# One batch's attention in whole float32, and a PSUM tile for each half of the experts' transposed rows

## The chip, the cores and the metric

The kernel runs on 1 core of one Trainium2 chip. The metric is the device time of one execution in microseconds (us); lower is better. A difference of 0.2% of the time is about what a measurement can tell from no change.

## The reference

```python
# 4 batches, 8 heads, 576 positions, head size 64
q_rot, k_rot = (rotate(q), rotate(k))                     # rotary embedding
scores = scale * np.matmul(q_rot, k_rot.transpose(0, 1, 3, 2))
scores = scores - np.max(scores, axis=-1, keepdims=True)
attn = np.exp(scores)
attn = attn / (np.sum(attn, axis=-1, keepdims=True) + 1e-09)
x = np.matmul(attn, v)                                    # then as 2304 rows of 512
# dense layer, 512 -> 2048 -> 512
h = x @ w_in
x = np.maximum(0.01 * h, h) @ w_out
# eight experts, each row goes to one
logits = xn @ en.T / tau                                  # rows and expert vectors of length 1
expert_idx = np.argmax(logits, axis=1)
for e in range(E):
    mask = expert_idx == e
    h = np.maximum(x[mask] @ w1[e], 0.0)
    out[mask] = gate_w[mask, None] * (h @ w2[e])
```

Inputs and output are float32.

## The kernel before, in words

**Parted numbers.** Nearly all matmuls take a float32 value as two narrower ones, a high part and the rest (low), and add up three products of the parts. ScalarE (ACT) makes a high part with a copy, VectorE (DVE) the low part with a subtraction.

**Attention.** The 16 pairs of heads (`g`: batch `g // 4`) have 9 units each (`u`), 144 in all. A unit is 128 queries of one head, the ninth one 64 queries of both heads. `prep(g)` makes a pair ready: it takes the sums of squares of q, k and v (`square`, ACT), turns q and k by the rotary tables (`rope_s2`, `rope_c2`, `add2`, DVE), sets scales, parts q and k into float16 (`hi`, `lo`) and has a DMA transpose put them into `stk`, d on the partitions. `prep_v` parts v. A unit then takes these steps: `a_scores` (PE, four float16 matmuls of 288 columns into the PSUM tile `S`), `a_max` (DVE, scaled scores to `E` with the row's extreme), `a_exp` (ACT), then the turned weights: `a_turn` (five PE transposes of `E` into the PSUM tile `acc`), `a_turned_hi` (ACT) and `a_turned_lo` (DVE) part them into `PT`; `a_pv` (15 float16 matmuls of 64 or 65 columns, 30 for the ninth unit) and `a_fin`. From the unit at which the dense layer starts, a DMA transposes the weights instead (`a_hi`, `a_lo`, `a_transpose`).

**Order.** The program is written in the order in which it runs on each engine. `step(i)` writes one step: the scores of unit i + 1, the maximum of unit i, the exponential and the turning of unit i - 1, the products of unit i - `LAG`. `ORDER1` is the order of the letters in a step ahead of the dense layer (X: `a_max`, E: `a_exp`, V: `a_pv`, T: `a_turn`, H and L: high and low part, C: `a_scores`, s and x: background pieces). Background jobs are the decoding of the dense weights (32 slices of 512 KB, `weights`), the preparation of the next pair and, later, x. A slice gets a piece in only when each engine's budget is above zero; `RATE1` adds to the budget at each step.

**Phases.** After a start of about 31 us, units 0 to 36 run with the decoding of the dense weights beside them. At unit 37 batch 0 is through and the dense layer's units (`m_s1`, `m_s2`) join. From about 780 us the experts run in 20 blocks of 128 rows (`e_block`). One block has `e_h` (24 PE matmuls, next block), `e_split` (the two weights parted again: 8 ACT copies, 8 DVE subtractions), `e_xt`, `e_relu`, `e_o` (24 matmuls), `e_weigh` and `e_tr`, which transposes the next block's hidden rows: four PE transposes for each half z, an ACT copy to `hth` and a DVE subtraction to `htl`. Both halves are written into one two-bank PSUM tile `acc`, and the framework tracks waits by the tile.

The lines to follow are L519 (`a_max`), L524 (`a_exp`), L543 (`a_turn`), L548 and L553 (high and low part of the turned weights), L567 (`a_pv`), L509 and L513 (`a_scores`), L427 and L493 (low parts in the preparation), and L917, L919, L925 (`e_tr`).

Of the kernel before, what the change touches and what calls it, by code (L numbers as in the profile page):

```python
# [32 lines left out]
LAG = 4  # L33
XTB = 2
# [4 lines left out]
EARLY = 2  # L39
# [8 lines left out]
RATE1 = dict(A=2.3, V=2.5)  # L48
# [44 lines left out]
def attention_moe_kernel(ctx: ExitStack, tc: tile.TileContext, qkv, w_in, w_out, emb, tau, w1, w2,  # L93
# [257 lines left out]
    v16s = [qkp.tile([128, 9, 2, 130], F16, name=f"v16{i}") for i in range(2)]  # L351
    pairs = {}
    xrow = {}

    def load(g, z):
        raws[g, z] = qkp.tile([128, z, 2, 5, 64], F32, name=f"raw{z}")
        for t in ([slice(0, 2)] if g else [slice(0, 1), slice(1, 2)]) if z == 2 else [slice(2, 3)]:
            if z == 2:
                M.loaded = M.tick
            if (g, z, t.start) == (0, 2, 1):  # L360
                nc.sync.dma_start(out=tab, in_=rope)
            nc.sync.dma_start(out=raws[g, z][:, t.start % 2:t.start % 2 + t.stop - t.start], in_=qkv[g, :, t])

    def prep(g):
        i0 = 9 * (g - 1)
        v16 = v16s[g % 2]
        raw, rawv = raws.pop((g, 2)), raws.pop((g, 1))[:, 0]
        sq = small.tile([128, 3], F32, name="sq3")
        cs, sn = tab[:, 0], tab[:, 1]
        if g:  # L370
            t4 = qkp.tile([128, 4, 5, 64], F32, name="t2", tag="stg")
        else:
            t2 = [mp.tile([128, 2, 5, 64], F32, name=f"t2{t}", tag="xT", bufs=XTB) for t in range(2)]

# [12 lines left out]

        def add(t):
            nc.vector.tensor_tensor(out=raw[:, t], in0=raw[:, t], in1=t2[t], op=ALU.add)

        r4 = raw.rearrange("p t h c d -> p (t h) c d")

        def rope_s2(z):
            o, i = 32 * z, 32 - 32 * z
            nc.vector.tensor_tensor(out=t4[:, :, :, o:o + 32], in0=r4[:, :, :, i:i + 32],
                                    in1=sn[:, :, o:o + 32].unsqueeze(1).to_broadcast([128, 4, 5, 32]), op=ALU.mult)

        def rope_c2():
            xf = raw.rearrange("p t h c d -> p (t h) (c d)")
            nc.vector.tensor_tensor(out=xf, in0=xf, in1=cs.rearrange("p c d -> p (c d)").unsqueeze(1).to_broadcast([128, 4, 320]), op=ALU.mult)  # L400

        def add2():
            rf = raw.rearrange("p t h c d -> p (t h c d)")
            nc.vector.tensor_tensor(out=rf, in0=rf, in1=t4.rearrange("p a c d -> p (a c d)"), op=ALU.add)
# [17 lines left out]
        def hi(out, t):  # L422
            nc.scalar.activation(out=out, in_=raw[:, t], func=AF.Copy, scale=s3[:, t:t + 1])

        def lo(out, t, high):
            for h in range(2):
                nc.vector.scalar_tensor_tensor(out=out[h], in0=raw[:, t, h], scalar=s3[:, t:t + 1], in1=high[:, h], op0=ALU.mult, op1=ALU.subtract)  # L427

        if g == 0:
            rope_s(1, nc.gpsimd)  # L430
            rope_s(0, nc.vector)
            for t in range(3):
                square(t)
            rope_c(0)
            add(0)
            pb = ps_x()
            nc.tensor.matmul(pb[:, 0:3], lhsT=ones, rhs=sq, start=True, stop=True)
            s3 = scales(pb)
            s2, qhi, khd, qlo, klo = stacks()
            hi(qhi, 0)  # L440
            rope_c(1)
            add(1)
            hi(khd[:, :, :, 0:64], 1)
            lo(qlo, 0, qhi)
            nc.vector.tensor_copy(out=khd[:, :, :, 64:128], in_=khd[:, :, :, 0:64])
            lo(klo, 1, khd[:, :, :, 0:64])
        else:
            yield Piece(A=0.93, V=0.73, at=max(i0 - EARLY, 0), tick=M.loaded + TLOAD)
            square(0)
            rope_s2(0)  # L450
            yield Piece(A=0.93, V=0.73)
            square(1)
            rope_s2(1)
            yield Piece(A=0.93, V=1.4)
            square(2)
            rope_c2()
            yield Piece(V=1.4)
            add2()
            pb = yield from total(sq, 3)
            yield Piece(must=True, V=0.6)  # L460
            s3 = scales(pb)
            s2, qhi, khd, qlo, klo = stacks()
            yield Piece(A=0.82)
            hi(qhi, 0)
            yield Piece(A=0.82, V=0.8)
            hi(khd[:, :, :, 0:64], 1)
            lo(qlo, 0, qhi)
            yield Piece(V=1.2)
            lo(klo, 1, khd[:, :, :, 0:64])
            nc.vector.tensor_copy(out=khd[:, :, :, 64:128], in_=khd[:, :, :, 0:64])  # L470
# [11 lines left out]
        pairs[g] = (stk, s3, sc, v16, zq[g % 2] if zq else None)  # L482
        if g + 1 < 4 * B:
            load(g + 1, 2)
        vjobs.append(Job(prep_v(g, v16, rawv, s3)))

    def prep_v(g, v16, rawv, s3):
        vh, vl = (v16[:, 0:5, :, o:o + 64].rearrange("p c h d -> p h c d") for o in (64, 0))
        yield Piece(A=0.82, at=9 * (g - 1) + LAG)
        nc.scalar.activation(out=vh, in_=rawv, func=AF.Copy, scale=s3[:, 2:3])  # L490
        yield Piece(V=0.75)
        for h in range(2):
            nc.vector.scalar_tensor_tensor(out=vl[:, h], in0=rawv[:, h], scalar=s3[:, 2:3], in1=vh[:, h], op0=ALU.mult, op1=ALU.subtract)  # L493
# [7 lines left out]
    def a_scores(g, u):  # L501
# [32 lines left out]
    def a_transpose(p):  # L534
        pt = ptp.tile([128, 10, 128], F16, name="PT")
        nc.sync.dma_start_transpose(out=pt[:, 0:9], in_=p)
        return pt, False
# [8 lines left out]
    def a_turned_hi(tf):  # L546
        pt = ptp.tile([128, 10, 128], F16, name="PT")
# [770 lines left out]
```

## Time and profile before

| | |
|---|---|
| time, median of 3 runs | 1089.99 us (1089.51 to 1091.2) |
| the profiled execution: its own time | 1091.79 us |
| its span | 1089.9 us |
| busy: PE matmul | 953.3 us (87%) |
| busy: PE weight load | 751.4 us (69%) |
| busy: DVE | 816.4 us (75%) |
| busy: ACT | 688.7 us (63%) |
| mean granted TensorE clock | 0.92 |

Busy times are shares of the whole span. The phases have different limits, so a share over the span does not say what a phase waits for.

### The profile page before, as it was taken

How to read it: one execution, taken by the hardware profiler on the slowest of the kernel's cores; microseconds unless marked ns; L12 is line 12 of the kernel's file. 1: busy time of each engine (PE TensorE's matmuls, PEld its weight loads, DVE VectorE, ACT ScalarE, POOL GpSimd, SP SyncE). 2: the span in 40 equal slices, each digit the busy share in tenths (PEclk: the TensorE clock that was granted, in tenths of full speed). 3: DMA queues.
4: the chain of work that ended last, by engine and by line, in shares of the span. 5: the costliest groups of instructions: out<-in, count | busy, mean ns of one | idle time of the engine just before them, and what ended most of it. 6: DMA issues, size and time to landing. Idle time of an engine off the chain costs nothing. (4 is left out here: it accounts for less than half of the span.)

```text
span 1089.9 us, 20159 instructions
## 1 busy us (share of the span) xinstructions
PE 953.3 (87%) x7427; PEld 751.4 (69%) x7427; DVE 816.4 (75%) x1663; ACT 688.7 (63%) x1105; POOL 53.3 (5%) x52
## 2 busy tenths in 40 slices
PE   1687787899997889998899999999987888888886
PEld 0354554576776677887788888888775777777774
DVE  6998888899877877897788765224757887777782
ACT  6767666677656655666675655232447777777772
POOL 1000000000000000000000000000003111111100
PEclk9956555699999889999999999999998999999998
DMA  8534426477567777667877844001430111133280
GB/s 243 154 79 155 134 66 188 87 160 150 111 136 159 122 150 152 139 129 155 151 136 142 143 78 85 20 21 42 162 115 31 49 40 39 39 99 124 75 292 13
DMA packets 232425, 124.41 MB, mean 114 GB/s; under 512 B 202616, under 2 KB 212216, under 8 KB 232321
## 3 DMA queue, kind: packets, MB, share of 16 engines
q1 hardware_dynamic: 229120, 113.10, 45.0%
q0 software_dynamic: 3200, 9.97, 2.6%
q8 instruction: 60, 0.98, 0.4%
q14 instruction: 45, 0.36, 0.1%
HBM read 120.04 MB, written 10.49 MB: 120 GB/s over the span
## 5 line engine op out<-in xcount | busy, mean ns | idle before, releaser
L248 PEld LDWEIGHTS <-wi 128*128 128x128 f16 x1920 | 171.4, 99 | 26.2 <-issue 4.2
L278 PE MATMUL acc<-wo,gh 128*128 128x512 f32 x576 | 156.9, 416 | 6.1 <-ACT gh L262 6.0
L519 DVE TENSOR_SCALAR_CACHE_REDUCE E<-S,sc 128x576 f32<-128x576 f32 x144 | 117.0, 813 | 38.5 <-PE S L511 27.6
L278 PEld LDWEIGHTS acc<-wo,gh 128*128 128x128 f32 x576 | 106.8, 195 | 31.2 <-ACT gh L262 8.5
L255 ACT ACTIVATE g<-h 128x512 f32<-128x512 f32 x72 | 43.0, 597 | 129.2 <-DVE gl L266 56.1
L567 PEld LDWEIGHTS <-PT 128*128 128x128 f16 (+1 forms) x2280 | 91.7, 107 | 34.7 <-issue 22.9
L248 PE MATMUL h<-xT,wi 128*128 128x256 f16 (+1 forms) x1152 | 113.4, 257 | 0.9 <-DMA xT<-x 0.9
L567 PE MATMUL o<-v,PT 128*128 128x65 f16 (+3 forms) x2280 | 105.9, 204 | 7.8 <-DMA PT<-P 7.8
L524 ACT ACTIVATE E<-E,amx 128x576 f32<-128x576 f32 x144 | 110.4, 767 | 3.6 <-DVE E L519 3.2
L509 PE MATMUL S<-stk 128*128 128x288 f16 (+1 forms) x320 | 94.5, 322 | 15.1 <-DVE E L519 14.4
L532 DVE SCALAR_TENSOR_TENSOR P<-E,P 128x576 f16<-128x576 f32 x108 | 81.2, 752 | 18.5 <-ACT P L528 18.2
L528 ACT ACTIVATE P<-E 128x576 f16<-128x576 f32 x108 | 73.8, 684 | 29.1 <-DMA PT<-P 25.8
L248 PE MATMUL h<-xt,wi 128*128 128x256 f16 x768 | 90.8, 276 | 0.4 <-DMA xt<-x 0.4
L278 PE MATMUL acc<-wo,gl 128*128 128x512 f32 x288 | 79.1, 397 | 0.0
L258 DVE SCALAR_TENSOR_TENSOR g<-h,g 128x512 f32<-128x512 f32 x72 | 49.5, 688 | 29.0 <-ACT g L255 28.9
L266 DVE TENSOR_TENSOR gl<-g,gh 128x512 fp32r<-128x512 f32 x72 | 49.4, 686 | 25.4 <-ACT gh L262 15.4
L543 PE MATMUL acc<-idn,E 128*128 128x128 f32 x180 | 46.2, 421 | 22.3 <-ACT E L524 15.9
L278 PEld LDWEIGHTS acc<-wo,gl 128*128 128x128 f32 x288 | 55.4, 193 | 12.8 <-DVE gl L266 0.3
L917 PE MATMUL acc<-idn,hs 128*128 128x128 f32 x160 | 25.7, 284 | 35.8 <-DVE htl L925 34.8
L935 PE MATMUL h<-w,hth 128*128 128x512 f32 x176 | 55.4, 396 | 0.0
L262 ACT ACTIVATE gh<-g 128x512 fp32r<-128x512 f32 x72 | 44.4, 617 | 15.1 <-PE acc L278 14.2
L925 DVE TENSOR_TENSOR htl<-acc,hth 128x512 fp32r<-128x512 f32 x40 | 27.5, 689 | 33.4 <-ACT hth L919 33.4
(237 smaller groups left out, 1869.0 us busy)
## 6 DMA issues: line engine op xcount, KB each, us to landing
rb<-in_w SPq DMA_DIRECT2D x78, 512.0 KB
ra<-in_w SPq DMA_DIRECT2D x76, 512.0 KB
raw<-in_qkv SPq DMA_DIRECT2D x15, 640.0 KB
raw<-in_w_in SPq DMA_DIRECT2D x16, 512.0 KB
raw<-in_w_out SPq DMA_DIRECT2D x16, 512.0 KB
raw<-in_qkv SPq DMA_DIRECT2D x18, 320.0 KB
x2s<-x SPq DMA_DIRECT2D x18, 256.0 KB
v<-v SPq DMA_DIRECT2D x16, 162.5 KB
```

What stands on the lines that cost most here:

```text
L248: nc.tensor.matmul(m.h[:, c0:c1], lhsT=wi[:, a, c, 128 * f:128 * f + 128], rhs=xT[j][:, 4 * b_ + c, 0:c1 - c0], start=(n == 0), stop=(n == ...
L258: nc.vector.scalar_tensor_tensor(out=m.g, in0=m.h, scalar=0.01, in1=m.g, op0=ALU.mult, op1=ALU.max)
L266: nc.vector.tensor_tensor(out=m.gl, in0=m.g, in1=m.gh.bitcast(F32), op=ALU.subtract)
L278: nc.tensor.matmul(M.acc[:, t], lhsT=g_[:, tt], rhs=wo[:, a, f], start=(f == 0 and n == 0), stop=(f == NF - 1 and n == 2))
L509: nc.tensor.matmul(ps[o:o + m, n, 0:288], lhsT=stk[:, h, c0:c0 + m], rhs=stk[:, 2 + h, ks], start=True, stop=False)
L519: nc.vector.tensor_scalar(out=e[:, 0:S].rearrange("p (a b) -> p a b", a=2), in0=ps[:, :, 0:288], scalar1=pairs[g][2][:, 1:2], scalar2=None ...
L524: nc.scalar.activation(out=e[:, 0:S], in_=e[:, 0:S], func=AF.Exp, scale=-1.0, bias=mx)
L528: nc.scalar.activation(out=p[:, 0:576], in_=e[:, 0:S], func=AF.Copy, scale=TWO15)
L532: nc.vector.scalar_tensor_tensor(out=p[:, 576:1152], in0=e[:, 0:S], scalar=TWO15, in1=p[:, 0:576], op0=ALU.mult, op1=ALU.subtract)
L543: nc.tensor.transpose(tf[:, 128 * i:128 * i + 128], e[:, 128 * i:128 * i + 128], idn)
L567: nc.tensor.matmul(o[ob:ob + m, 256 * h:256 * h + w], lhsT=pt[:, i, q0:q0 + m], rhs=v16[:, j, h, c:c + w], start=(n == 0), stop=(n == len( ...
L935: nc.tensor.matmul(OP[kk], lhsT=h_[:, c, :], rhs=wt[a][c // 2][:, 512 * (c % 2):512 * (c % 2) + 512], start=(n == 0), stop=(n == len(todo) ...
```

## The change

For the pairs of the first batch (`g < WHOLE`, 36 units) q, k, v and the exponentials stay float32: `prep_whole` takes the place of `prep`, without squares, scales, parts and DMA transpose. It turns q and k with ten PE transposes and three ACT copies. `load_values` loads v as it is, with the column of ones beside it. A score is one float32 matmul, the turned weights are one ACT copy (`a_turned`), and `a_pv` has 5 float32 matmuls. The layout of q, k, v in memory is changed (blocks of positions ahead of heads), so the rotary products have other shapes for all pairs. `RATE1` is raised from 2.3 and 2.5 to 2.4 and 2.7. In `x_done` a doubling moves into the scale of the square. In `e_tr` each half has a one-bank PSUM tile of its own (`ps_o`, two buffers).

```diff
+WHOLE = 4
-RATE1 = dict(A=2.3, V=2.5)
+RATE1 = dict(A=2.4, V=2.7)
...
+    def load_values(g):
+        yield Piece(at=9 * (g - 1) + LAG)
+        v = values[g] = stp.tile([128, 1170], F32, name="v32", tag="v")[:, 0:650].rearrange("p (c h x) -> p c h x", c=5, h=2)
+        nc.gpsimd.memset(v[:, :, :, 64:65], 1.0)
+        nc.sync.dma_start(out=v[:, :, :, 0:64], in_=qkv[g, :, 2])
...
+    def ropes(raw):
+        t4 = qkp.tile([128, 2, 5, 2, 64], F32, name="t2", tag="stg")
+        cs, sn = (tab[:, i].unsqueeze(2).to_broadcast([128, 5, 2, 64]) for i in range(2))
+
+        def rope_s(t):
+            for z in range(2):
+                o, i = 32 * z, 32 - 32 * z
+                nc.vector.tensor_tensor(out=t4[:, t, :, :, o:o + 32], in0=raw[:, t, :, :, i:i + 32], in1=sn[:, :, :, o:o + 32], op=ALU.mult)
+
+        def rope_c(t):
+            nc.vector.tensor_tensor(out=raw[:, t], in0=raw[:, t], in1=cs, op=ALU.mult)
...
+    def prep_whole(g):
+        i0 = 9 * (g - 1)
+        raw = raws.pop((g, 2))
+        qk = stp.tile([128, 1600], F32, name="qk", tag="stk")[:, 0:1280].rearrange("p (t x) -> p t x", t=2)
+
+        def turn(t, pt):
+            for c in range(4):
+                nc.tensor.transpose(pt[:, 128 * c:128 * c + 128], raw[:, t, c].rearrange("p h d -> p (h d)"), idn)
...
+        def keep(t, pt):
+            nc.scalar.activation(out=qk[:, t, 0:512], in_=pt, func=AF.Copy)
...
+            yield Piece(V=0.85, at=max(i0 - EARLY, 0), tick=M.loaded + TLOAD)
+            rope_s, rope_c, add = ropes(raw)
+            rope_s(0)
+            yield Piece(V=0.85)
+            rope_s(1)
+            yield Piece(V=1.5)
+            rope_c(0)
+            rope_c(1)
+            yield Piece(V=1.4)
+            add(slice(0, 2))
+            for t in range(2):
+                yield Piece(x=True)
+                pt = ps_x()
+                turn(t, pt)
+                yield Piece(must=True, A=0.6)
+                keep(t, pt)
...
             for h, c0, m, o in todo:
                 hr = slice(64 * h, 64 * h + 64)
+                if g < WHOLE:
+                    nc.tensor.matmul(ps[o:o + m, n, 0:288], lhsT=stk[hr, 0, c0:c0 + m], rhs=stk[hr, 1, ks], start=True, stop=True)
+                    continue
...
-    def a_turned_hi(tf):
-        pt = ptp.tile([128, 10, 128], F16, name="PT")
-        nc.scalar.activation(out=pt[:, 0:5].rearrange("p i q -> p (i q)"), in_=tf, func=AF.Copy, scale=TWO15)
-        return pt, True
-
-    def a_turned_lo(tf, pt):
-        hi, lo = (pt[:, z:z + 5].rearrange("p i q -> p (i q)") for z in (0, 5))
-        nc.vector.scalar_tensor_tensor(out=lo, in0=tf, scalar=TWO15, in1=hi, op0=ALU.mult, op1=ALU.subtract)
+    def a_turned(tf):
+        pt = ptp.tile([128, 5, 128], F32, name="ET", tag="PT")
+        nc.scalar.activation(out=pt.rearrange("p i q -> p (i q)"), in_=tf, func=AF.Copy)
+        return pt
...
+        if g < WHOLE:
+            todo = [(i, i, 0, 65) for i in range(5)]
...
-        pa = ps_a()
         for z in range(2):
-            pt = pa[:, z]
+            pt = ps_o()
...
-        turn = not (M.unit or m_ready())
+        turn = prv and units[i - 1][0] < WHOLE
```

In PE's queue, one step of the units of batch 0 (S is the score tile, acc the turned exponentials, o the products, E the exponentials) stood so; 15 pairs of a weight load and a product follow, of which two stand here:

```order
L543 MATMUL acc<-idn,E_117 128x128 x5
L509 LDWEIGHTS stk
L509 MATMUL S<-stk 128x288
L513 LDWEIGHTS stk
L513 MATMUL S<-stk 128x288
L509 LDWEIGHTS stk
L509 MATMUL S<-stk 128x288
L513 LDWEIGHTS stk
L513 MATMUL S<-stk 128x288
L567 LDWEIGHTS PT
L567 MATMUL o<-v_122,PT 128x65
```

Now the same place has these rows, with the transposes of the next pair's q or k (raw) among them:

```order
L583 MATMUL acc<-idn,E_117 128x128 x5
L404 MATMUL t<-idn,raw_177 128x128 x2
L547 MATMUL S<-qk 128x288 x2
L603 MATMUL o<-v_129,ET 128x65 x5
L583 MATMUL acc<-idn,E_118 128x128 x5
```

Four score matmuls have become two and 15 products five, all in float32, and ten transposes for each pair are new on PE.

In DVE's queue, the steps between two maxima (L519) at units 4 to 6 stood so (raw, wi, wo: decoding of the dense weights; v: low part of v; PT: low part of the turned weights):

```order
L519 TENSOR_SCALAR E_117,amx<-S,sc 128x576
L493 SCALAR_TENSOR_TENSOR v_123<-raw_203,ps,v_123 128x5x64 x2
L553 SCALAR_TENSOR_TENSOR PT<-acc,PT 128x640
L86 TENSOR_SCALAR pt<-t 128x1
L87 TENSOR_SCALAR ps<-pt 128x1
L88 TENSOR_SCALAR uw<-pt 128x1
L519 TENSOR_SCALAR E_118,amx<-S,sc 128x576
L226 SCALAR_TENSOR_TENSOR wi<-raw_310,ps,wi 128x4x128
L192 SCALAR_TENSOR_TENSOR raw_348<-raw_348 128x512
L553 SCALAR_TENSOR_TENSOR PT<-acc,PT 128x640
L194 SCALAR_TENSOR_TENSOR raw_348<-raw_348 128x512
```

Now there stand at units 3 to 5, with L559 as the maximum:

```order
L559 TENSOR_SCALAR E_118,amx<-S 128x576
L193 SCALAR_TENSOR_TENSOR raw_293<-raw_293 128x512
L195 SCALAR_TENSOR_TENSOR raw_293<-raw_293 128x512
L559 TENSOR_SCALAR E_117,amx<-S 128x576
L193 SCALAR_TENSOR_TENSOR raw_316<-raw_316 128x512
L195 SCALAR_TENSOR_TENSOR raw_316<-raw_316 128x512
L87 TENSOR_SCALAR pt<-t 128x1
L88 TENSOR_SCALAR ps<-pt 128x1
L89 TENSOR_SCALAR uw<-pt 128x1
L559 TENSOR_SCALAR E_118,amx<-S 128x576
```

The parting of the turned weights and of v is gone from a step, and the decoding stands a little earlier among the units.

In PE's queue at an expert block's `e_tr` (the end of `e_o`, the two halves, the start of `e_h`), with what each row waits for, stood:

```order
L935 MATMUL h<-v2h_10178,htl 128x512
L917 MATMUL acc<-idn,hs 128x128 [waits Activation_49]
L917 MATMUL acc<-idn,hs 128x128 x3
L917 MATMUL acc<-idn,hs 128x128 [waits DVE_49]
L917 MATMUL acc<-idn,hs 128x128 x3
L900 MATMUL S<-v1h_10167,exh 128x512 [waits Activation_49]
```

Now there stand:

```order
L970 MATMUL h<-v2h_9650,htl 128x512
L952 MATMUL o<-idn,hs 128x128 [waits Activation_49]
L952 MATMUL o<-idn,hs 128x128 x3
L952 MATMUL o<-idn,hs 128x128 [waits PE_49,Activation_49]
L952 MATMUL o<-idn,hs 128x128 x3
L936 MATMUL S<-v1h_9639,exh 128x512 [waits Activation_49]
```

The second half's transposes no longer wait for DVE.

## Rows read from the trace of the kernel before

**Rows 1.** The page's 40 slices (tenths): DVE, and the granted TensorE clock.

```profile
DVE  6998888899877877897788765224757887777782
PEclk9956555699999889999999999999998999999998
```

**Rows 2.** Windows: us, PE, PEld, DVE, ACT, POOL busy; clock, DMA share, GB/s.

```profile
90.00:120.00 30.00, 25.94 (x163) 16.43 (x163) 26.10 (x62) 21.17 (x39) 0.00 (x0) 0.50 0.20 59
950.00:1000.00 50.00, 45.25 (x218) 36.97 (x217) 39.98 (x40) 39.30 (x51) 7.08 (x7) 1.00 0.36 122
```

**Rows 3.** Timeline of DVE: the maxima of units 0 and 36.

```profile
31.26 0.81 DVE L519 TENSOR_SCALAR_CACHE_REDUCE E<-S,sc 128x576 f32<-128x576 f32 x1
...
202.38 0.81 DVE L519 TENSOR_SCALAR_CACHE_REDUCE E<-S,sc 128x576 f32<-128x576 f32 x1
```

**Rows 4.** Groups by form, window 31.2 to 205 us.

```profile
L553 DVE SCALAR_TENSOR_TENSOR PT<-acc,PT 128x640 f16<-128x640 f32 x35 | 28.7, 821 | 10.2 <-ACT PT L548 10.2
L194 DVE SCALAR_TENSOR_TENSOR raw<-raw 128x512 uint32<-128x512 uint32 x23 | 15.8, 687 | 0.2
L427 DVE SCALAR_TENSOR_TENSOR stg<-raw,ps,stg 128x320 f16<-128x320 f32 x18 | 9.1, 546 | 0.0
L226 DVE SCALAR_TENSOR_TENSOR wi<-raw,ps,wi 128x512 f16<-128x512 f32 x11 | 8.2, 748 | 0.2
L548 ACT ACTIVATE PT<-acc 128x640 f16<-128x640 f32 x36 | 24.8, 689 | 8.4 <-PE acc L543 8.4
L376 ACT ACTIVATE junk<-raw 128x640 fp8e4<-128x640 f32 x14 | 10.2, 729 | 0.1
```

**Rows 5.** Timeline of PE around a rise and a fall of the clock.

```profile
165.20 1.30 PE L543 MATMUL acc<-idn,E 128*128 128x128 f32 x5 [0.36 <-DVE PT L553]
166.44 0.40 PE L509 MATMUL S<-stk 128*128 128x288 f16 x1
166.77 0.42 PE L513 MATMUL S<-stk 64*128 64x288 f16 x1
...
167.83 1.85 PE L567 MATMUL o<-v,PT 128*64 128x65 f16 x30
...
172.05 0.62 PE L567 MATMUL o<-v,PT 128*128 128x65 f16 x15
176.01 1.33 PE L543 MATMUL acc<-idn,E 128*128 128x128 f32 x5 [3.33 <-ACT E L524]
```

**Rows 6.** Windows of 2 us at the same place, columns as in rows 2.

```profile
170.00:172.00 2.00, 2.00 (x9) 0.97 (x7) 1.18 (x5) 0.87 (x2) 0.00 (x0) 0.53 1.00 346
172.00:174.00 2.00, 0.68 (x16) 0.51 (x15) 1.52 (x3) 1.03 (x2) 0.00 (x0) 1.00 1.04 370
176.00:178.00 2.00, 1.99 (x9) 1.59 (x9) 1.11 (x3) 2.00 (x4) 0.00 (x0) 0.50 0.00 0
```

**Rows 7.** Timeline of PE at the full clock: scores, and small float32 matmuls.

```profile
127.68 0.28 PE L509 MATMUL S<-stk 128*128 128x288 f16 x1
127.90 0.29 PE L513 MATMUL S<-stk 64*128 64x288 f16 x1
...
522.54 1.04 PE L330 MATMUL t<-enT,x2T 128*128 128x8 f32 x8
523.43 0.28 PE L509 MATMUL S<-stk 128*128 128x288 f16 x1
```

**Rows 8.** Timeline of the start: the DMA transpose on SP's queue, and DVE's wait.

```profile
13.90 3.96 SPq L473 DMA_TRANSPOSE stk<-stg  x1
22.46 0.39 SPq L211 DMA_DIRECT2D raw<-in_w_in  x1
28.59 0.69 DVE L192 SCALAR_TENSOR_TENSOR raw<-raw 128x512 uint32<-128x512 uint32 x1 [2.41 <-ACT raw L190]
```

**Rows 9.** Timeline of one expert block, from one transposition to the next.

```profile
960.59 0.60 PE L917 MATMUL acc<-idn,hs 128*128 128x128 f32 x4
...
974.69 0.60 PE L917 MATMUL acc<-idn,hs 128*128 128x128 f32 x4
975.48 0.59 ACT L919 ACTIVATE hth<-acc 128x512 fp32r<-128x512 f32 x1
976.14 0.69 DVE L925 TENSOR_TENSOR htl<-acc,hth 128x512 fp32r<-128x512 f32 x1
976.88 0.66 PE L917 MATMUL acc<-idn,hs 128*128 128x128 f32 x4 [1.59 <-DVE htl L925]
977.29 0.70 PE L900 MATMUL S<-w1h,exh 128*128 128x512 f32 x2
```

**Rows 10.** PE's waits: window 780 to 870 us, then 870 to 1089 us.

```profile
PE acc L917 <- DVE htl L925: 11.1, 4, 6.5
...
PE acc L917 <- DVE htl L925: 23.7, 15, 1.6
```

More of the change, by code (lines that the diff above doesn't have):

```diff
@@ L350, in attention_moe_kernel @@
     raws = {}
-    v16s = [qkp.tile([128, 9, 2, 130], F16, name=f"v16{i}") for i in range(2)]
-    pairs = {}
+    pairs, values = {}, {}
     xrow = {}
     def load(g, z):
-        raws[g, z] = qkp.tile([128, z, 2, 5, 64], F32, name=f"raw{z}")
+        raws[g, z] = qkp.tile([128, z, 5, 2, 64], F32, name=f"raw{z}")
         for t in ([slice(0, 2)] if g else [slice(0, 1), slice(1, 2)]) if z == 2 else [slice(2, 3)]:
@@ L422, in hi @@
         def hi(out, t):
-            nc.scalar.activation(out=out, in_=raw[:, t], func=AF.Copy, scale=s3[:, t:t + 1])
+            nc.scalar.activation(out=out, in_=by_head[:, t], func=AF.Copy, scale=s3[:, t:t + 1])
         def lo(out, t, high):
             for h in range(2):
[L427 to L470, printed above, removed]
@@ L471, in prep @@
+        add(slice(0, 2))
+        pb = yield from total(sq, 3)
+        yield Piece(must=True, V=0.6)
+        s3 = scales(pb)
+        s2, qhi, khd, qlo, klo = stacks()
+        yield Piece(A=0.82)
+        hi(qhi, 0)
+        yield Piece(A=0.82, V=1.0)
+        hi(khd[:, :, :, 0:64], 1)
+        lo(qlo, 0, qhi)
+        yield Piece(V=1.3)
+        lo(klo, 1, khd[:, :, :, 0:64])
+        nc.vector.tensor_copy(out=khd[:, :, :, 64:128], in_=khd[:, :, :, 0:64])
         yield Piece(at=i0 - 1)
@@ L979, in jobs @@
     def jobs():
-        if (L.prep is None or not L.prep.live) and preps and (preps[0], 1) in raws:
-            L.prep = Job(prep(preps.popleft()))
+        if (L.prep is None or not L.prep.live) and preps and all((preps[0], z) in raws for z in ((2,) if preps[0] < WHOLE else (1, 2))):
+            L.prep = Job((prep_whole if preps[0] < WHOLE else prep)(preps.popleft()))
         for q in (xjobs, vjobs, rjobs):
@@ L1019, in step @@
         slot(must=True)
-        turn = not (M.unit or m_ready())
+        turn = prv and units[i - 1][0] < WHOLE
         second = M.second
-        for z in ORDER1 if rate is RATE1 and turn else ORDER_B if second else ORDER_A:
+        for z in ORDER1 if rate is RATE1 and (turn or not m_ready()) else ORDER_B if second else ORDER_A:
             if z == "E" and prv:
                 a_exp(*e_[i - 1])
-            elif z == "T" and prv:
+            elif z == "T" and turn:
                 tf = a_turn(e_[i - 1][0])
```

144 lines of the change are left out of this document (81 added, 63 removed).

## The prediction

> **What bounds the kernel now.** The slices come first, for the phases. DVE is near 9 tenths up to about slice 25, and the granted clock shows a hole in slices 3 to 8 [rows 1]. Those slices are units 0 to 36, where the change sits. The windows then give each phase's engines. Between 90 and 120 us DVE is busy 87%, PE 86% and ACT 71%, at a clock of 0.50; between 950 and 1000 us, among the expert blocks, PE has 90%, DVE 80%, ACT 79%, at a clock of 1.00 [rows 2].
>
> In the units the maximum of unit 0 starts at 31.26 us and that of unit 36 at 202.38 us, so 36 steps take 171.1 us, 4.75 us each [rows 3]. To see which engine sets them I went through the queues of DVE and ACT from one maximum (one exponential) to the next, and gave each instruction the mean of its group, of which the large ones are in [rows 4]. DVE comes to 165 us over the 36 steps, ACT to 135 us, and when the longer of the two is taken in each step the sum is 172 us, against 171.1 measured. So a step lasts as long as the fuller of these two queues, and mostly that is DVE. PE, at the low clock, needs 1.24 us for the five transposes (165.20 to 166.44), 1.4 us for four score matmuls (0.35 from one to the next) and 0.9 us for the 15 products (half of the 30 in 1.85) [rows 5]: 3.5 us, which fits into 4.75.
>
> In the expert phase PE is the bound. From one `e_tr` to the next there are 14.10 us (960.59 to 974.69). Inside, the first half's transposes start at 974.69, ACT copies, DVE subtracts to 976.83, and only then the second half starts, at 976.88, with 1.59 us shown as PE's wait for DVE [rows 9]. Over the phase these waits are 11.1 + 23.7 = 34.8 us in 19 cases, the longest 6.5 us [rows 10].
>
> **The change part by part.**
>
> *The start: 2 us less.* The DMA transpose held SP's queue for 3.96 us, and the fifth weight slice was issued at 22.46. Its landing set ACT, for which DVE waited 2.41 us ahead of unit 0's maximum [rows 8]. The transpose, pair 0's parts and scales are gone, and the loads behind them may go out earlier; but a slice's buffer comes free only when its decoding is done. So at least 0, at most those 3.96 + 2.41 = 6 us; I take 2, nearer to 0, because the decoding ahead is untouched.
>
> *The units, DVE and ACT.* Gone from DVE are 36 low parts of 0.821 us (30 us) and 12 of q and k, of 0.546 (three pairs that fall into this stretch, 7 us); low parts of v, copies and scales are another 7 us by the same count. Added are three weight slices that the new order brings ahead of unit 37 (each two operations like L194 and one like L226, 2.1 us, 6 us in all) and about 6 us of smaller operations that move in from the neighbouring steps or get more pieces in the rotary products: 165 - 44 + 12 is about 134 us. ACT loses nine squares of 0.729 and six copies of q and k, and gets copies out of PSUM and the three slices: 133 us. The new copy of 640 float32 values I price as L548, 0.689 us [rows 4]. The longer of the two in each step now gives 156 us, 15 less than before. DVE's wait for ACT ahead of the low part (10.2 us, [rows 4]) is gone too, but lay inside those steps.
>
> *The units, PE.* This is the open price: no row has a wide float32 matmul. The nearest is L330: four float32 matmuls of 8 columns, which stand as eight instructions and take 0.89 us at the full clock (522.54 to 523.43), 0.11 each [rows 7]. So five products of 65 columns are ten instructions, 1.1 us at the full clock and 2.2 at half. For a score of 288 columns the float16 row is the lower bound of each of its two instructions: 0.22 us at the full clock (127.68 to 127.90, [rows 7]) and 0.35 at the low one [rows 5]. The upper bound is twice that, since a small float32 matmul at 0.11 us also takes about twice the 0.06 us that the low clock's float16 product takes, or more. Four of them cost 0.9 to 1.8 us, or 1.4 to 2.8 us; I take the middle. With the transposes (0.6 or 1.24) and the pair's ten new ones (0.14 or 0.28 a step) a step needs 3.2 us of PE at the full clock (2.8 to 3.6), hidden under 156 / 36 = 4.3 us, and 5.8 us at the low one (5.1 to 6.5), not hidden. The page "FP8 and Floating Point Precision" of the Trainium skill (TensorE Precision Notes) has true float32 as four passes through the array; by that, as an estimate, four instructions of two passes would make 1.0 us of scores at the full clock, and the sum would be the same within 0.3 us a step. No run here shows it yet.
>
> So the clock decides. In the rows it rose after a dense stretch of PE (170 to 172 us: 2.00 of 2.00 busy, 0.53, then 1.00) and fell after 3.33 us of waiting for an exponential, behind a long preparation step [rows 5, 6]. The new low-clock step, at 5.8 us, leaves PE no gap, which by these rows should raise the clock; the long preparation steps, five among the 36 by the queues (about 7 us of DVE each), should let it fall again. For each fall I charge one step at 5.8 instead of 3.8 us, 2 us, 10 in all: 166 us, 5 less than before. Range of this term: 15 less (clock never matters) to 36 x 6.5 = 234 us, 63 more.
>
> *Units after 36: 3 us less.* The three slices brought forward leave 2.1 us each on DVE there. PE has its dense matmuls in that stretch, so between 0 and 6; I take half. The doubling that `x_done` saves and the other rotary shapes lie under PE's work there: nothing, and a few tenths a pair if DVE were the bound.
>
> *The experts: 34 us less.* With its own tile the second half starts behind the first, 0.44 us later (the second follows its wait at 976.88 with the next `e_h` at 977.29, so four transposes take about 0.41) and not 2.19 us later: 1.75 us for each of 17 blocks, 30 us. The wait of 6.5 us is in the setup of the third block, where PE would go on with `e_h` while DVE is late with other work; I take 3, as DVE and ACT stay as late as they are. The first two transpositions give about 1. What is late next: a block falls to 12.35 us. DVE does 39.98 / 50 x 14.1 = 11.3 us in it and ACT 11.1 [rows 2], so both fit, with a slack of 1 us. The second half's `htl` is needed only half-way through the following `e_o`, behind `e_h`'s 5 us. Bounds: 17 (half, if ACT or DVE begin to hold PE) and 36.
>
> *Sum.* 1091.8 - 2 - 5 - 3 - 34 = 1047.8 for the profiled execution. That execution is 1.8 us above the median of the runs, so 1046 on the scale of the median.
>
> **The rivals.**
>
> *The clock stays low throughout the units.* For it: the window from 90 to 120 us has PE 86% busy at 0.50 [rows 2]. Against it: a fully dense stretch did raise it [rows 6]. Then a step is PE's 5.8 us: 36 x 5.8 = 209, 38 more, and the kernel ends near 1089 (1064 to 1114 over the price of the scores). From 171.1 + 39 = 210 us, or 5.8 us a step, the change is lost; above that it is slower. This is the case on the other side, and the price of a 288-column float32 matmul, 0.5 us an instruction, is its turning point. The page "TensorE: Matmul & The Clock Gate" of the Trainium skill (Part 4) says that transposes do not count as busy for the clock, and each step here has five to nine; by that rule this rival would be the outcome. The trace leaves it open: the rise came in a stretch that had transposes and 30 products. Chance 20%, half of it slower or within 0.2%.
>
> *The clock stays high.* If gaps remain under the 3.33 us of the fall, the units take 156 us and the kernel 1036. For it: the expert phase holds 1.00 at 90% busy [rows 2]. Against it: the long preparation steps remain. 15%.
>
> *The experts give half.* ACT and DVE have 1 us of slack in a block; if their chain over `e_relu` and `e_split` holds PE, or the expert weights land too late for the shorter block, 17 us are lost: 1063. 12%.
>
> **How the numbers follow.** The forecast has 48%, the three rivals 20, 15 and 12, and 5 are left for something else. Its own range is 1036 to 1056. Up to 1082 it takes in the third rival and most of the first, down to 1030 the second with the start's bound: 8 in 10. A measurement can tell 0.2% (2 us). Faster: 48 + 15 + 12, 10 of the first rival and 3 of the rest, 88%; within 0.2%: 3%; slower: 9%.
>
> **What would show it.** In the profile of the changed kernel: unit 0's maximum at about 29 us and unit 36's 166 us behind it; a granted clock that goes up and down within the first 200 us, with DVE no longer the fuller engine; `e_tr`'s second half within 0.5 us of the first, and blocks of 12.4 us. A block of 13 us or more would contradict the expert term, and a PE busy throughout at a clock of 0.5 the units' term. The prediction goes wrong first of all through the cost of the float32 scores and through the clock.

## The result, and the profile after

The changed kernel takes 1042.32 us (median of 4 runs, 1038.69 to 1047.76) against 1090.23 us for the kernel before beside it: ratio 0.9564 [0.9519, 0.9609]. The profiled execution took 1038.69 us, with a span of 1036.8 us. The runs of the changed kernel lie 9 us apart, those of before 2 us (5 at most on the chips of the experiments); what may lie behind that comes below.

The page's slices of DVE and of the granted clock, to be laid beside [rows 1]:

```profile
DVE  5667559778779868887987967422566999899992
PEclk9999558599999799999999999999999999999998
```

DVE is no longer near 9 tenths in the first fifth; the clock still has a hole there. Next, the maxima of units 0 and 36 in DVE's timeline, which answer to [rows 3]:

```profile
29.11 0.75 DVE L559 TENSOR_SCALAR_CACHE_REDUCE E<-S 128x576 f32<-128x576 f32 x1
...
200.71 0.82 DVE L559 TENSOR_SCALAR_CACHE_REDUCE E<-S,sc 128x576 f32<-128x576 f32 x1 [0.50 <-PE S L553]
```

Unit 0 comes 2.15 us earlier, but the 36 steps behind it take 171.6 us, where they took 171.1. The window of these steps in the kernel before (columns as in [rows 2]):

```profile
31.26:202.38 171.12, 134.96 (x909) 84.67 (x909) 148.69 (x343) 117.22 (x207) 0.00 (x0) 0.62 0.42 119
```

And two windows of the changed kernel: the same steps, and a piece of them.

```profile
29.11:200.71 171.60, 164.78 (x748) 126.15 (x747) 118.78 (x301) 117.22 (x204) 0.35 (x3) 0.79 0.35 107
110.00:158.00 48.00, 48.00 (x180) 37.20 (x181) 26.71 (x69) 27.43 (x49) 0.12 (x1) 0.50 0.31 94
```

Over the steps DVE's busy time fell by 30 us, and PE's rose by as much. In the piece PE is busy for 48.00 of 48.00 us, DVE and ACT for little over half, and the clock stays at 0.50. PE's timeline shows the price of a step there, and at 1.00:

```profile
91.73 1.33 PE L603 MATMUL o<-v,ET 128*128 128x65 f32 x10
92.90 0.72 PE L583 MATMUL acc<-idn,E 128*128 128x128 f32 x5
93.45 0.28 PE L182 MATMUL t<-wsq,ones 128*128 128x1 f32 x2
93.66 1.23 PE L547 MATMUL S<-qk 64*128 64x288 f32 x4
94.83 0.88 PE L603 MATMUL o<-v,ET 128*128 128x65 f32 x6
...
118.35 2.39 PE L603 MATMUL o<-v,ET 128*128 128x65 f32 x10
120.54 1.27 PE L583 MATMUL acc<-idn,E 128*128 128x128 f32 x5
121.61 0.63 PE L404 MATMUL t<-idn,raw 128*128 128x128 f32 x2
122.17 2.29 PE L547 MATMUL S<-qk 64*128 64x288 f32 x4
124.38 2.39 PE L603 MATMUL o<-v,ET 128*128 128x65 f32 x10
```

From one start to the next, products cost 1.17 and 2.19 us, transposes 0.55 and 1.07, scores 1.17 and 2.21: a step is 3.1 us of PE at the full clock (91.73 to 94.83) and 6.03 here at the half one, with two of the pair's transposes in it. A score instruction is 0.29 and 0.55 us.

In the experts, PE's timeline has both halves of `e_tr` as one group of eight, answering to [rows 9]:

```profile
885.65 1.04 PE L952 MATMUL o<-idn,hs 128*128 128x128 f32 x8
886.44 0.71 PE L936 MATMUL S<-w1h,exh 128*128 128x512 f32 x2
...
897.93 1.03 PE L952 MATMUL o<-idn,hs 128*128 128x128 f32 x8
```

A block is 12.28 us in place of 14.10. PE's largest waits from 780 us to the end, answering to [rows 10]:

```profile
PE S L936 <- ACT exh L924: 1.0, 1, 1.0
PE h L970 <- DVE htl L960: 1.0, 1, 1.0
PE h L970 <- ACT eo L976: 0.9, 1, 0.9
```

The 34.8 us of waiting for `htl` are gone. From the first `e_h` weight load to the end there are 267.6 us in place of 305.7. Behind unit 36 the profiles differ as well: windows from unit 36's maximum to unit 140's, of before and then of after.

```profile
202.38:643.97 441.59, 416.94 (x4085) 336.23 (x4086) 358.09 (x848) 285.08 (x492) 0.00 (x0) 0.96 0.72 139
```

```profile
200.71:628.87 428.16, 410.32 (x4071) 336.42 (x4072) 349.27 (x837) 276.85 (x476) 1.29 (x11) 0.97 0.72 141
```

That is 13.4 us less, with 8.8 us less of DVE's work. So the profiled execution gained 2 at the start, nothing in the units, 13 behind them and 38 in the experts: 53 us, as the two spans differ (1089.9 to 1036.8).

### The profile page after: what moved, and what is told of

It reads as the page before. It is cut to its first block, busy times and chain, and to the rows that moved or that the text cites. A ratio compares the mean times of both kernels' runs of the same rounds, so it can differ in the third digit from the quotient of the medians.

```text
span 1036.8 us, 19801 instructions
## 1 busy us (share of the span) xinstructions
PE 974.7 (94%) x7259; PEld 794.2 (77%) x7259; DVE 771.0 (74%) x1596; ACT 674.2 (65%) x1081; POOL 64.3 (6%) x64
## 5 line engine op out<-in xcount | busy, mean ns | idle before, releaser
L279 PE MATMUL acc<-wo,gh 128*128 128x512 f32 x576 | 154.2, 410 | 1.5 <-ACT gh L263 1.4
L559 DVE TENSOR_SCALAR_CACHE_REDUCE E<-S,sc 128x576 f32<-128x576 f32 x108 | 87.8, 813 | 42.8 <-PE S L551 27.5
L603 PEld LDWEIGHTS <-PT 128*128 128x128 f16 (+1 forms) x1680 | 61.4, 100 | 23.3 <-issue 14.9
L603 PEld LDWEIGHTS o<-v,ET 128*128 128x128 f32 (+1 forms) x400 | 61.6, 244 | 20.0 <-issue 19.9
L603 PE MATMUL o<-v,PT 128*128 128x65 f16 (+3 forms) x1680 | 69.9, 194 | 5.3 <-DMA PT<-P 5.3
L547 PE MATMUL S<-qk 64*128 64x288 f32 (+1 forms) x160 | 67.8, 613 | 0.8 <-DVE E L559 0.7
L549 PE MATMUL S<-stk 128*128 128x288 f16 (+1 forms) x240 | 60.9, 293 | 7.5 <-DVE E L559 7.5
L603 PE MATMUL o<-v,ET 128*128 128x65 f32 (+1 forms) x400 | 67.4, 335 | 0.0
L559 DVE TENSOR_SCALAR_CACHE_REDUCE E<-S 128x576 f32<-128x576 f32 x36 | 27.2, 754 | 37.2 <-PE S L547 37.1
```

Of the source, the lines that this page charges most:

```text
L279: nc.tensor.matmul(M.acc[:, t], lhsT=g_[:, tt], rhs=wo[:, a, f], start=(f == 0 and n == 0), stop=(f == NF - 1 and n == 2))
L547: nc.tensor.matmul(ps[o:o + m, n, 0:288], lhsT=stk[hr, 0, c0:c0 + m], rhs=stk[hr, 1, ks], start=True, stop=True)
L603: nc.tensor.matmul(o[ob:ob + m, 256 * h:256 * h + w], lhsT=pt[:, i, q0:q0 + m], rhs=v[:, j, h, c:c + w], start=(n == 0), stop=(n == len(to ...
```

## The experiments

Times are medians of four runs (ten for `e10`), the ratio is to the kernel before on the same chip; the other columns come from the profiled execution (maxima of units 0, 36 and 140 in DVE's timeline, DVE's busy time in the window of the last two).

| kernel | us | ratio | units 0-36 | units 36-140 | DVE there |
|---|---|---|---|---|---|
| before | 1090.2 | 1 | 171.1 | 441.6 | 358.1 |
| after | 1042.3 | 0.9564 | 171.6 | 428.2 | 349.3 |
| e1 experts' edit alone | 1052.4 | 0.9659 | 171.4 | 439.3 | 357.9 |
| e2 experts' edit undone | 1084.1 | 0.9941 | 176.7 | 430.7 | 349.2 |
| e3 f16 in a single pass | 1013.6 | 0.9307 | 142.2 | 429.7 | 349.1 |
| e4 two bursts | 1057.3 | 0.9686 | 183.5 | 435.8 | 349.2 |
| e5 6 fillers a unit | 1019.4 | 0.9361 | 144.5 | 431.7 | 349.2 |
| e6 turned by matmul | 1026.4 | 0.9421 | 148.3 | 438.5 | 349.5 |
| e7 doubling back | 1042.5 | 0.9570 | 172.5 | 430.2 | 350.9 |
| e8 rates back | 1043.4 | 0.9573 | 173.8 | 430.6 | 350.1 |
| e9 3 fillers a unit | 1031.5 | 0.9448 | 163.9 | 428.4 | 349.4 |
| e10 before, by matmul | 1094.6 | 1.0034 | 175.5 | 440.1 | 358.1 |
| e11 low rates | 1052.4 | 0.9641 | 178.4 | 433.9 | 355.8 |
| e12 DVE's work back | 1040.7 | 0.9559 | 157.7 | 438.4 | 358.8 |

**The two halves of the change apart.** e1 is the kernel before with only

```diff
-        pa = ps_a()
         for z in range(2):
-            pt = pa[:, z]
+            pt = ps_o()
```

> The kernel before with one edit: the experts' transposed rows go to a PSUM tile per half. Theory (the parts add up, and the experts' block is 12.3 us with this edit alone): 16 blocks give 1.8 us each, the third block's setup 6, the first two 2.4, so about 38 us off 1090: 1050 to 1055, with the maxima of the attention units where they were before (202 at unit 36, 784 at the first relu). Rival (the shorter block also needs the changed attention, by the clock or by what is left over from the earlier stages): blocks of 13 to 14 us and 1065 to 1085.

Measured 1052.41 us, 0.9659 [0.9643, 0.9675]: the theory. e2 is the changed kernel without it.

> The changed kernel with the experts' transposed rows back in one PSUM tile of both halves. Theory (the parts add up): blocks of 14.1 us again and 38 us more than the changed kernel: 1078 to 1083, so the attention's part alone is worth 8 to 15 us. Rival (the attention's part is worth nothing by itself): 1088 to 1092.

Measured 1084.09 us, 0.9941 [0.9921, 0.9961], just past the theory's 1083 and below the predicted gain of 8 to 15: whole float32 attention, with the smaller edits that go with it, is alone worth 5 us. PE's waits from 775 us on show the old wait again:

```profile
PE acc L953 <- DVE htl L961: 34.6, 19, 6.5
```

So 37 of the 48 us come from three lines in the experts, and the large edit brings the small part. The two alone add up to 42; the 5 to 6 us that are missing lie within the spread of the changed kernel's runs.

**What bounds the units.** e3 narrows the first batch's tiles:

```diff
-qk = stp.tile([128, 1600], F32, ...)      # q, k turned
+qk = stp.tile([128, 3200], F16, ...)
-v = values[g] = stp.tile([128, 1170], F32, ...); nc.sync.dma_start(...)
+v = values[g] = stp.tile([128, 2340], F16, ...); nc.gpsimd.dma_start(...)
-pt = ptp.tile([128, 5, 128], F32, name="ET", tag="PT")
+pt = ptp.tile([128, 5, 128], F16, name="ET", tag="PT")
```

> The changed kernel with q, k, v and the softmax weights of the first batch rounded to f16 (no low parts, so its result is less exact): scores and products run as f16 in a single pass, all else is the same. Theory (in the first batch's 36 steps TensorE is the bound, at 5.8 us for a step at half clock, and the DVE and ACT work of 134 and 133 us lies under it): a step of TensorE falls to 1.4 us at full and 2.6 us at half clock, and units 0 to 36 take 135 to 155 us in place of 171.6; the whole kernel ends 15 to 35 us earlier, at 1008 to 1028. Rival (the chain score, maximum, exponential, transposes and copy sets the step, whatever TensorE's price): units 0 to 36 stay at 165 to 172 us and the time at 1036 to 1046.

Measured 1013.55 us, 0.9307 [0.9288, 0.9325], units 0 to 36 in 142.2 us: the theory. DVE and ACT did the same work (117.0 and 116.9 us busy there, 118.8 and 117.2 before this edit), so it was PE's price that went with the 29 us (the load of v also moves from SP's queue to GpSimd's). Groups by form of PE from 40 to 170 us in that run; the last number ahead of the second bar is the mean of one instruction in ns, which overlaps with its neighbours:

```profile
L583 PE MATMUL acc<-idn,E 128*128 128x128 f32 x170 | 45.2, 432 | 40.2 <-ACT E L564 40.2
L547 PE MATMUL S<-qk 64*128 64x288 f16 x58 | 19.0, 430 | 1.9 <-DVE E L559 1.9
```

PE now waits 40 us for the exponential, and its transposes still run at half speed (432 ns): at the half clock PE's share of a step now fits under DVE and ACT.

**Why the clock stays low.** Work of another kind was put in, first in two places:

```diff
+                if i in (6, 15):
+                    hot, heat = ps_h(), ones.bitcast(F16)
+                    for k in range(24):
+                        nc.tensor.matmul(hot[:, 0:256], lhsT=heat[:, 0:128], rhs=heat, start=(k == 0), stop=(k == 23))
                 ps_[i + 1] = a_scores(*units[i + 1])
```

> The changed kernel with 24 added f16 matmuls of 128x256 into an unused PSUM tile, ahead of the scores of unit 7 and again of unit 16; nothing reads them. Theory (TensorE's clock stays at 0.5 through 48 us without a gap because the work there is float32 matmuls and transposes, and it is raised by a dense stretch of f16 work, as at 206 to 208 us in the midst of 24 such matmuls): the clock rises in or right behind each burst, steps after them take 3.7 us in place of 5.8, and units 0 to 36 take 150 to 165 us with the bursts' own 5 to 10 us in it; the time is 1025 to 1038. Rival (what is streamed does not matter, the clock rises at its own times): units 0 to 36 take 174 to 182 us, and the time is 1045 to 1053.

Measured 1057.30 us, 0.9686 [0.9653, 0.9718]; units 0 to 36 in 183.5 us, past the rival's 182. Yet the clock did answer. PE's timeline at the first burst, and two windows 10 us later:

```profile
60.31 1.27 PE L583 MATMUL acc<-idn,E 128*128 128x128 f32 x5
61.38 4.33 PE L1103 MATMUL h<-ones 128*128 128x256 f16 x24
65.64 1.23 PE L547 MATMUL S<-qk 64*128 64x288 f32 x4
66.80 1.33 PE L603 MATMUL o<-v,ET 128*128 128x65 f32 x10
67.97 0.72 PE L583 MATMUL acc<-idn,E 128*128 128x128 f32 x5
```

```profile
76.00:80.00 4.00, 2.80 (x9) 1.60 (x10) 3.75 (x10) 2.90 (x6) 0.00 (x0) 0.77 0.00 0
80.00:84.00 4.00, 4.00 (x19) 3.69 (x19) 2.44 (x7) 1.71 (x3) 0.00 (x0) 0.50 0.71 194
```

Transposes go from 1.27 to 0.72 us across the burst, and the clock falls at the next preparation step, where DVE (3.75 of 4 us) holds PE up. The second burst, at 104.68 us, found the clock already up: it had risen near 95 us, among the ordinary steps. Neither theory was right: the clock rises in the first burst, but is lost again at the next preparation step. Two further kernels act in every unit. In e5:

```diff
             elif z == "T" and turn:
+                hot, heat = ps_h(), ones.bitcast(F16)
+                for k in range(6):
+                    nc.tensor.matmul(hot[:, 0:256], lhsT=heat[:, 0:128], rhs=heat, start=(k == 0), stop=(k == 5))
                 tf = a_turn(e_[i - 1][0])
```

> The changed kernel with 6 added f16 matmuls of 128x256 into an unused PSUM tile ahead of the transposes of every unit of the first batch; nothing reads them. In the run with two bursts such matmuls took 0.12 us each at full and 0.22 us at half clock, and the clock rose in both bursts (rows of the full clock stand right behind each), but fell again about 10 us later, where DVE and ACT held TensorE up. Theory (f16 work in the holes that DVE and ACT leave keeps the clock up): a step of 3.1 + 0.7 us at full clock, units 0 to 36 in 140 to 160 us in place of 171.6, the time 1010 to 1032. Rival (the clock falls all the same, at the holes that are left): most steps at 5.8 + 1.3 us, units 0 to 36 in 180 to 215 us, the time 1050 to 1085.

Measured 1019.44 us, 0.9361 [0.9346, 0.9377], units 0 to 36 in 144.5 us: the theory. The kernel with the added, unread work is 23 us faster than the one without. e6 adds nothing, but replaces the transposes in `a_turn`:

```diff
-            nc.tensor.transpose(tf[:, 128 * i:128 * i + 128], e[:, 128 * i:128 * i + 128], idn)
+            nc.tensor.matmul(tf[:, 128 * i:128 * i + 128], lhsT=e[:, 128 * i:128 * i + 128], rhs=idn, start=True, stop=True)
```

> The changed kernel with the five transposes of a unit's softmax weights as plain float32 matmuls against the identity (same result in PSUM). A product of 65 columns takes 0.22 us at half clock, so one of 128 about 0.43, where the transpose takes 0.21: a unit's five cost 2.1 us in place of 1.07 at half clock, 1.1 in place of 0.55 at full. Theory A (the transposes are what the clock does not count as work, and keep it at half): it rises within some 10 us of dense work and comes back soon after each hole; steps of 3.7 to 4 us, units 0 to 36 in 140 to 165 us, the time 1012 to 1036. Theory B (float32 scores and products do not raise it either): most steps at 6.9 us, units 0 to 36 in 190 to 235 us, the time 1060 to 1105.

Measured 1026.40 us, 0.9421 [0.9378, 0.9464], units 0 to 36 in 148.3 us: theory A. PE's timeline of that run, early in the units:

```profile
43.95 2.50 PE L583 MATMUL acc<-idn,E 128*128 128x128 f32 x10
46.25 0.63 PE L404 MATMUL t<-idn,raw 128*128 128x128 f32 x2
46.81 1.60 PE L547 MATMUL S<-qk 64*128 64x288 f32 x4
48.34 1.33 PE L603 MATMUL o<-v,ET 128*128 128x65 f32 x10
```

Turning a unit's weights costs 2.30 us here (1.17 at the full clock), twice the transposes' price, and still the clock rises early: the scores at 46.81 are the first to shorten, the products at 48.34 stand at the full clock. In the changed kernel rows at half speed went on to 81 us. Its rise there, and its two falls:

```profile
79.64 1.89 PE L547 MATMUL S<-qk 64*128 64x288 f32 x4
81.45 1.33 PE L603 MATMUL o<-v,ET 128*128 128x65 f32 x10
...
108.63 1.11 PE L400 MATMUL t<-idn,raw 128*128 128x128 f32 x4 [1.14 <-DVE pt L87]
...
180.66 1.33 PE L583 MATMUL acc<-idn,E 128*128 128x128 f32 x5 [1.44 <-ACT E L564]
```

It rose in the midst of dense steps with transposes and float32 products, and so it did at 159 us. What let it rise just then, after 45 to 50 us of such steps at half speed, is not settled. Windows of e6 at a preparation step, and of the changed kernel at one:

```profile
68.00:72.00 4.00, 2.66 (x18) 2.08 (x17) 3.93 (x9) 1.58 (x3) 0.00 (x0) 1.00 0.00 0
72.00:76.00 4.00, 3.29 (x26) 2.77 (x24) 3.46 (x9) 2.53 (x6) 0.00 (x0) 1.00 0.43 118
```

```profile
104.00:108.00 4.00, 3.04 (x23) 2.02 (x21) 3.97 (x7) 2.67 (x5) 0.00 (x0) 1.00 0.00 0
108.00:112.00 4.00, 3.37 (x9) 1.99 (x9) 3.85 (x13) 3.20 (x7) 0.00 (x0) 0.54 0.00 0
```

PE is busy for 5.95 of 8 us in the one and for 6.41 in the other: with the larger holes, e6 keeps its 1.00 (its transposes of q and k at 70.25 us stand at the full clock's price), and the kernel with transposes falls. e9 asks how little filler is enough (`range(3)` for `range(6)`):

> The changed kernel with 3 added f16 matmuls of 128x256 ahead of a unit's transposes in place of the 6 of the run before (0.35 us at full clock). Theory (a step at full clock is set by DVE and ACT at about 4.1 us, and a little work that is not a transpose is enough to keep the clock up): units 0 to 36 take 140 to 150 us as with 6, the time is 1012 to 1026. Rival (it takes the 6): holes bring the clock down again, units 0 to 36 take 152 to 180 us, the time 1024 to 1052.

Measured 1031.53 us, 0.9448 [0.9419, 0.9478], units 0 to 36 in 163.9 us: the rival. The recorded clock fell near 67, 102, 146 and 190 us and came back each time before the next of these; windows of the second fall:

```profile
96.00:100.00 4.00, 2.76 (x22) 2.13 (x22) 3.93 (x8) 1.88 (x4) 0.00 (x0) 1.00 0.00 0
100.00:104.00 4.00, 3.73 (x18) 3.00 (x17) 3.93 (x11) 3.55 (x7) 0.00 (x0) 0.72 0.03 5
104.00:108.00 4.00, 4.00 (x16) 3.10 (x13) 0.75 (x2) 2.31 (x4) 0.00 (x0) 0.50 0.83 258
```

Three fillers did not keep the clock up at such a hole.

e10 puts e6's edit into the kernel before:

> The kernel before with the five transposes of a unit's softmax weights as float32 matmuls against the identity (1.33 us at full clock for a unit in the changed kernel's run of this edit, 2.50 at half). Theory (the kernel before is bound by DVE in these units, 157 of 180 us busy, whatever the clock): the clock stands higher, but units 0 to 36 still take 160 to 175 us in place of 171, and the time is 1078 to 1095. Rival (the half clock also sets the step of the kernel before): units 0 to 36 take 140 to 155 us and the time is 1060 to 1074.

Measured 1094.59 us, 1.0034 [1.0018, 1.0050], units 0 to 36 in 175.5 us, half a microsecond past the theory's range: the theory, against the rival's 140 to 155. Windows from 50 to 170 us of before, and of e10:

```profile
50.00:170.00 120.00, 98.20 (x699) 62.74 (x699) 104.83 (x240) 82.68 (x143) 0.00 (x0) 0.58 0.43 123
```

```profile
50.00:170.00 120.00, 93.79 (x806) 69.27 (x806) 103.35 (x237) 82.23 (x142) 0.00 (x0) 0.82 0.41 116
```

The clock goes from 0.58 to 0.82, and the units gain nothing: they take 4 us more, with DVE busy as before (104.83 and 103.35 us). The low clock was there before the change too, and raising it in this way paid only once PE set the step. That it cost nothing at all before is argued, not shown, since e10 also doubles the price of each turning.

**What the stage behind unit 36 gained.** Two edits of the change were undone alone. e7 has the doubling in `x_done` back:

```diff
-        nc.scalar.activation(out=junk[:, 0:512], in_=x, func=AF.Square, scale=2.0 ** 0.5, ...)
-        yield Piece(V=0.5)
+        nc.scalar.activation(out=junk[:, 0:512], in_=x, func=AF.Square, ...)
+        yield Piece(V=0.3)
+        nc.vector.tensor_scalar(out=sq, in0=sq, scalar1=2.0, scalar2=None, op0=ALU.mult)
```

> The changed kernel with the doubling of a finished row block's sum of squares back in a DVE instruction of its own (and its smaller planned cost), as before the change. Theory (the 13 us that units 36 to 140 gained lie in where SP's queue happens to stand when its transposes land, not in this edit): units 36 to 140 take 426 to 433 us and the time is 1038 to 1050. Rival (this edit carries them): 437 to 442 us and 1050 to 1057.

> The changed kernel with the planner's old rates for the first stage (2.3 and 2.5 us of pieces per step in place of 2.4 and 2.7). Theory (the first stage is bound by TensorE, so that the place of the pieces does not matter there, and the middle's gain is not theirs): units 0 to 36 take 168 to 178 us, 36 to 140 426 to 436, and the time is 1036 to 1050. Rival (the new rates carry the middle's gain, by having the weights done earlier): units 36 to 140 take 437 to 445 us and the time is 1050 to 1060.

Measured 1042.51 us, 0.9570 [0.9523, 0.9618], and, with `RATE1 = dict(A=2.3, V=2.5)`, 1043.44 us, 0.9573 [0.9549, 0.9597]: in both, units 36 to 140 stayed at 430 us, so neither edit alone carries the gain. e11 sets `RATE1 = dict(A=2.2, V=2.3)`, so that decoding is left over as in the kernel before:

> The changed kernel with the planner's rates for the first stage at 2.2 and 2.3 us of pieces per step: four pieces of the weights' decoding are then left for units 39 to 50, and a dense unit's turn is missed at unit 53, much as in the kernel before; all else is the changed kernel. Theory (what units 36 to 140 gained is the weights' decoding, 7 us of DVE, and the dense work that no longer waits for it): units 36 to 140 take 435 to 443 us in place of 428 to 432, and the time is 1046 to 1058. Rival (it is not the decoding): units 36 to 140 take 426 to 434 us and the time is 1036 to 1050.

Measured 1052.36 us, 0.9641 [0.9582, 0.9700], but for another reason than expected: units 36 to 140 took 433.9 us (the rival's range), and it was units 0 to 36 that took 178.4. e12 adds e7's edit to e11's, and the second DVE instruction for v's low parts:

```diff
-        nc.vector.scalar_tensor_tensor(out=vl, in0=rv, ..., in1=vh, ...)
+        for h in range(2):
+            lo_h, hi_h = (v16[:, 0:5, h, o:o + 64] for o in (0, 64))
+            nc.vector.scalar_tensor_tensor(out=lo_h, in0=rawv[:, :, h], ..., in1=hi_h, ...)
```

> The changed kernel with three things as they were: the planner's rates at 2.2 and 2.3 us (four pieces of the weights' decoding left for the stage behind unit 36), the doubling in an instruction of its own, and the low parts of v in two DVE instructions, one per head. DVE's busy time between units 36 and 140 should then be about 358 us, as before the change (349 in the changed kernel, 356 with the rates alone). Theory (what that stage gained is DVE's work, all of it together): units 36 to 140 take 436 to 443 us, as the 439 to 442 of the kernel before. Rival (it is not the work, but where the transposes land in SP's queue): 426 to 434 us, as in the other kernels with the change.

Measured 1040.70 us, 0.9559 [0.9512, 0.9607]. Units 36 to 140 took 438.4 us with DVE at 358.8, in the theory's range, in one profile. But the loss does not stand where the kernel before has it. That kernel lost to the changed one at units 60 to 68 (33.3 against 31.3 us) and 100 to 116 (71.8 against 66.8), and there e12 took 32.4 and 68.0; what it lost lies at units 52 to 60 (37.3 against 34.2) and 76 to 84 (38.0 against 34.0). So e12 does not show that DVE's work is the cause. Its whole time shows none of this loss, since units 0 to 36 took 157.7 us in that run.

## Why the prediction was right, and where it was not

The forecast of 1046 us holds (1042.3 measured). Its sum does not hold term by term: errors of both signs cancelled, so that it came so close is in part luck.

*The start*, 2 us less: 2.15 measured.

*The units, DVE and ACT*: 15 us off DVE and ACT's longer queue. e5 and e6 bear it out and show more: with the clock up the 36 steps take 144 to 148 us, below the 156 of the count. The change in DVE's work was right (31 us less by the count, 30 by the windows), the level was not: the counts of 165 and 134 us stand against 148.69 and 118.78 busy, and ACT's 135 and 133 against 117.22 both times. So the 172 that matched the measured 171.1 was too good a match, and the 156 built in the same way came out as an upper bound.

*The units, PE*: the price of a step was right, 3.2 and 5.8 us forecast, 3.1 and 5.8 measured (products started at 46.82, 52.64 and 58.46 us). So was the score at the middle of its bounds: 0.29 and 0.55 us an instruction. What failed is the sentence that the new low-clock step "leaves PE no gap, which by these rows should raise the clock", and with it the 10 us for five falls (each priced at 5.8 less 3.8 us, where the prediction's own count has 4.3 for a step at the full clock). A dense stretch at half clock lasted 48 us. Nor did a fall need a wait of 3.33 us, as the second rival took it: the two in the changed kernel came behind waits of 1.14 and 1.44 us. In the profiled execution 17 of the 36 steps took over 5.2 us, 101 us together (five such steps remain in e5, at the preparations), and the other 19 took 3.7 us each. The term came out at 0 where 5 were forecast. The rival "the clock stays low throughout" was half true. The rule that went with it, from "TensorE: Matmul & The Clock Gate" of the Trainium skill (Part 4: transposes do not count as busy for the clock), is what e6 shows: five transposes fewer in a unit, their work done by matmuls at twice the time each, and the clock is up. It is not the whole account, as the clock of the changed kernel also rose at 81 and 159 us with the transposes in place. The rise that I set against this rival ([rows 5, 6]) was no evidence against the rule, since the 30 products in that stretch are f16 matmuls and not transposes. How the moments of the falls shift from run to run also fits the scatter of 9 us: with the same order in the units, or nearly, 0 to 36 took 171.6, 176.7 and 172.5 us (after, e2, e7), and with the clock held, in e5, the runs still lie 6 us apart. That the clock alone makes the scatter is argued, not shown, and the recorded mean clocks do not settle it: in the changed kernel the longest run has the lowest (0.941 at 1047.8 us, 0.951 at 1038.7), in e11 the highest (0.961 at 1057.4, 0.951 at 1044.0).

*Units after 36*, 3 us less: 13.4 in the profile. The term was mis-sized. The nine kernels with DVE at 349 to 351 us there average 431.5 us, the four at 358 to 359 average 439.9. That would make DVE's 8.8 us worth about 8, where I had let PE's work cover most of it. But this is a comparison, not a cause shown: three of the four are the kernel before in these units, the fourth is e12, whose loss stands elsewhere, and the nine spread from 428.2 to 438.5. A rival stands untested: the new layout of q, k and v, with its loads and rotary products, which no run undoes. About 5 us seem to belong to this execution: from unit 76 to 80 the kernel before took 24.2 us, this one 18.8, but e6, with the change, 25.5; in each, ACT waits there for a DMA transpose of x (9.0, 4.2 and 9.1 us). What sets the length of that wait was not settled, and the cause of the rest stays open.

*The experts*, 34 us less: 38.1 in the profile, 37 by e1 alone. The mechanism was the one described; 16 blocks gained 1.8 us each (29, forecast 30 over 17 blocks), the third block's setup gave 6 in place of 3, since its whole wait of 6.5 us went, and the first two transpositions gave 2.5 in place of 1. DVE and ACT kept under the shorter block (11.18 and 10.82 of 12.28 us busy, from 885.65 us), against the third rival.

For the profiled execution the sum was 9 us too high (1047.8 against 1038.69): 5 forecast in the units that did not come, 14 too few behind them and in the experts. Against the median it is 4, as the profiled execution is the fastest of the four.

## What to carry to other kernels

Before PE takes over work from DVE, price it at the clock that this stretch really gets, and look at what PE does there: where transposes are part of its queue, a busy PE was no sign of a full clock here. If PE then sets the step, turning by a matmul against the identity can pay although each costs double (1042 to 1026 us here; in the kernel before, where PE did not set the step, it cost 4), and so can filler in its holes (1019, the fastest kernel here that computes in whole float32). Look also for two halves of a job in one tile: the wait that such a tile makes cost 37 us here, seven times what the rest of the change alone brought.

## What the runs showed of the hardware

In the profiles looked at, the granted clock stands at 1.00 from the start until its first recorded change, whatever the rows say. Groups of PE in the changed kernel by form, from 38 to 80 us (recorded 1.00) and from 110 to 158 us (0.50):

```profile
L547 PE MATMUL S<-qk 64*128 64x288 f32 x27 | 15.7, 725 | 0.0
L583 PE MATMUL acc<-idn,E 128*128 128x128 f32 x40 | 10.3, 420 | 0.1
...
L547 PE MATMUL S<-qk 64*128 64x288 f32 x32 | 18.3, 724 | 0.0
L583 PE MATMUL acc<-idn,E 128*128 128x128 f32 x40 | 10.2, 419 | 0.0
```

The same durations, so these units began at half clock; in e3 the whole of units 0 to 36 ran so under a recorded 1.00. So a mean that reaches into that time, such as the 0.79 of units 0 to 36 above, is too high. Here the durations of a known instruction tell the level, the clock column only its changes. Work that nobody reads made a kernel 2% faster (e5), and work of the same kind in two bursts made it 1.4% slower (e4).
